# The products that only keep TensorE at work: three F32R products for each fp32 one

## The chip, the cores and the metric

The kernel runs on one core of one Trainium2 chip. The metric is the device time of one execution in microseconds; it is given as the median of several runs. [...] A product in fp32 runs on TensorE as two passes, each with its own weight load, and the trace shows both; a product in F32R (fp32 bits, rounded beforehand) is one pass.

## The reference, cut to what matters

Two parts, the second fed by the first, for 4 batches, 8 heads of 48, 768 steps, model width 384 and inner width 1024:

```python
f = 1.0 / (1.0 + np.exp(-f_logit))
for t in range(S):                                   # gated linear attention
    state = f[:, :, t, :, None] * state + np.einsum('bhd,bhe->bhde', k[:, :, t], v[:, :, t])
    y[:, :, t] = np.einsum('bhd,bhde->bhe', q[:, :, t], state)
...
k = np.maximum(xk @ w_k, 0.0)                        # xk, xr: x mixed with the step before
v = k * k @ w_v
r = 1.0 / (1.0 + np.exp(-(xr @ w_r)))
return (r * v).astype(np.float32)
```

## The kernel before

**Work.** The attention runs in 24 chunks of 128 steps (`YA`, `YB`, `SP`, `TR` or `QT` and others are the TensorE tasks of a chunk: many small products of 64 x 64, lines 373, 393, 410, transposes at 344 and 351). Three chunks make a unit of 384 steps, and there are 8 units. A unit's mixing network is `F` (xk times w_k, 8 blocks), `R` (xr times w_r, 3 blocks) and `W` (squares times w_v, 6 half blocks), all in `mm3` at line 558: each fp32 operand is split into a high and a low F32R part, and three products of 384 columns (high-high, high-low, low-high) stand for one.

**Weights.** They come as 64-bit words. For each piece DVE turns the words into fp32 in three steps (`S`, `T`, `X`: lines 678, 687, 690), ACT rounds the high part (`H`, line 693) and POOL subtracts it for the low part (`L`, line 697). `k.w["wv"]` is a pair of tiles, [0] for high and [1] for low parts, of 8 blocks of 384 columns. The last block of the second tile is filled by the pieces `wvL4` and `wvL5`, which run after 50 us.

**Order.** The string `ORDER` gives one sequence of all tasks, and `emit` pins each engine to it: an engine never runs a task ahead of one that stands before it. A token such as `+4s` is a filler: `fill` issues that many products of constants, whose result nobody reads. Its letter says into which part of PSUM they go: `y` (`py`), `s` (`pss`) or `m1` (tile 1 of `pm`). In order, the fillers are `+2y +1y +1y` in the first 12 us and `+1m1 +2s +4s +2m1 +1s` between 34 and 44 us: 14 fp32 products of 256 columns, for which the trace shows 28 passes.

**Start of the program.** DVE sets `sure`, `low` (a tile of 512 columns: column 0 of each block of 128 is 1, the rest 1e-18), `py` and `pss`. Then it starts on `sf0.0` (line 463), which waits for the first DMA of `f`.

**Names in the steps below.** `zb` (line 330) and `T` (336) are DVE steps of the attention's state, after `SP` (lines 373 and 393) of their chunk. `F0.0` is the first block of unit 0's network: the first product of line 558 in the trace. It needs a PSUM tile that the weight piece `wv3` leaves at its `X` step (line 690).

Of the kernel before, what the change touches and what calls it, by code (L numbers as in the profile page):

```python
# [17 lines left out]
DM, DFF = 384, 1024  # L18
P = 128
# [7 lines left out]
NF = DFF // P  # L27
# [165 lines left out]
FL = "p a c -> p (a c)"  # L193
# [3 lines left out]
class Rwkv:  # L197
# [554 lines left out]
    def fill(self, what):  # L752

        count, bank = int(what[0]), what[1:]
        to = (self.py[:, 0, 256:] if bank == "y" else self.pss[:, 0, :256] if bank == "s"
              else self.tiles["pm"][int(bank[1:])][:, :256])
        for _ in range(count):
            self.nc.tensor.matmul(to, self.low[:, 0], self.low[:, 1:3], start=False, stop=True, skip_group_check=True)

    def add_start(self, pl):  # L760
        nc = self.nc
# [64 lines left out]
@with_exitstack  # L826
def rwkv_kernel(ctx: ExitStack, tc: tile.TileContext, zt, qkt, vt, wk, wr, wv, mu, cst, gen, out):
    nc = tc.nc
    k = Rwkv(nc, tc)
    k.zt, k.qkt, k.vt, k.wk, k.wr, k.wv, k.mu, k.cst = zt, qkt, vt, wk, wr, wv, mu, cst  # L830
    cp = ctx.enter_context(tc.tile_pool(name="cp", bufs=1))
    pm = ctx.enter_context(tc.tile_pool(name="pm", bufs=1, space=bass.MemoryType.PSUM))


    k.f_t = [cp.tile([P, UC, NP, C], F32, name=f"f{i}") for i in range(NFB)]
    k.qk_t = [cp.tile([P, 2, NP, C], F32, name=f"qk{i}") for i in range(NQ)]
    k.ident = cp.tile([P, P], F32, name="ident")
    k.tri = cp.tile([P, P], F32, name="tri")
    k.sure = cp.tile([P, 1], F32, name="sure")
    k.mask = cp.tile([P, C // 2], F32, name="mask")  # L840
    k.mu_sb = cp.tile([P, 2, KJ], F32, name="mu_sb")
    k.one_mu = cp.tile([P, 2, KJ], F32, name="one_mu")
    k.z_t = [[cp.tile([P, NP, 64], F32, name=f"z{i}{h}") for h in (0, 1)] for i in range(2)]
    k.done = cp.tile([P, 2], F32, name="done")
    k.sm = cp.tile([P, NP, D], F32, name="sm")
    k.low = cp.tile([P, NP, C], F32, name="low")
    k.g_t = cp.tile([P, 2, NP], F32, name="g")
    k.bl = cp.tile([P, N, NP], F32, name="bl")
    k.w = {
        n: [cp.tile([P, a, b], F32R, name=f"{n}{i}") for i in (0, 1)]  # L850
        for n, a, b in (("wk", KJ, DFF), ("wr", KJ, DM), ("wv", NF, DM))
    }

    k.pss = pm.tile([P, 2, 512], F32, name="pss")

    k.py = pm.tile([P, 2, 512], F32, name="py")
    k.least = cp.tile([P, 15], F32, name="least")
    k.flag = cp.tile([1, 1], I32, name="flag")
    k.tiles = {
        tag: [  # L860
            (pm if tag == "pm" else cp).tile([P] + shape, F32R if tag[:2] in ("xh", "xl") else F32, name=f"{tag}{i}")
            for i in range(n)
        ]
        for tag, (n, shape) in BUFS.items()
        if not tag.startswith("k2")
    }

    k.turns = ctx.enter_context(tc.tile_pool(name="turns", bufs=1))
    k.words = {
        tag: k.turns.tile([P, KJ, 2 * P, 2], I32, name=f"words_{tag}", tag=tag) for tag in BUFS if tag.startswith("k2")  # L870
    }
    nc.scalar.preload_act_table_set(EXP_SET)
    nc.vector.memset(k.sure, FULL)
    for r in (0, 64):
        nc.vector.memset(k.sure[r : r + D], SURE)
    nc.vector.memset(k.low, LOW)
    nc.vector.memset(k.low[:, :, 0:1], 1.0)
    nc.vector.memset(k.py[:, :, :], 0.0)
    nc.vector.memset(k.pss[:, :, 256 : 256 + NP * D], 0.0)
    for t in (*k.z_t[0], *k.z_t[1]):  # L880
        nc.gpsimd.memset(t[:, :, D:], 0.0)

    plan = Plan()
    k.add_start(plan)
    k.add_all(plan, lambda u, t: out[u // NU, u % NU * UT + t * P : u % NU * UT + t * P + P, :])
    k.emit(plan.schedule())
    with tc.If(k.strong > 0):
        general(k, gen, out)
# [121 lines left out]
```

## Time and profile before

| | |
|---|---|
| median of 3 runs | 341.58 us (341.30 to 341.67) |
| the profiled execution | 341.73 us |
| its span, first to last instruction | 339.9 us |
| mean granted clock of TensorE | 0.999 |
| PE / DVE / ACT / POOL busy | 94% / 75% / 60% / 45% |

The profiled execution is 1.8 us longer than its span, and 0.15 us above the median. Times in the rows below count from the start of the span.

### The profile page before, as it was taken

The numbers are of one execution on the slowest core, as the hardware profiler recorded it, in microseconds if no ns is written. First come the engines' busy times: TensorE is split into PE (matmuls) and PEld (weight loads), VectorE is DVE, ScalarE is ACT, GpSimd is POOL, SyncE is SP. The second block draws the span as 40 slices with busy tenths as digits, with TensorE's granted clock in tenths as the row PEclk, the third lists the DMA queues.
The fourth block names the chain that finished last, engine by engine and source line by source line (L and its number), as shares of the span: only waits on it lengthen the run. The fifth ranks groups of instructions, "written<-read, shape, count | busy, mean of one in ns | idle before, by whom it ended". The sixth has DMA issues, their size and how long they took to land. (4 is left out here: it accounts for less than half of the span.)

```text
span 339.9 us, 10992 instructions
## 1 busy us (share of the span) xinstructions
PE 320.8 (94%) x4574; PEld 304.5 (90%) x4574; DVE 255.5 (75%) x519; ACT 205.2 (60%) x432; POOL 153.4 (45%) x194
## 2 busy tenths in 40 slices
PE   4795889999999999999999999999999999999993
PEld 4675678899999999999999999999999999999993
DVE  5997999999988987686998886787475627837420
ACT  3888788784887736783658648591858236133420
POOL 2369589847762435313653356525612405214300
PEclk9999999999999999999999999999999999999999
DMA  7999667015465234470257122541520133040002
GB/s 230 398 385 360 185 193 273 14 29 158 175 198 152 75 97 153 102 267 25 87 125 269 62 46 85 170 143 60 187 91 5 32 117 92 35 141 23 0 4 79
DMA packets 20347, 45.24 MB, mean 133 GB/s; under 512 B 2752, under 2 KB 12736, under 8 KB 20288
## 3 DMA queue, kind: packets, MB, share of 16 engines
q1 hardware_dynamic: 20144, 44.25, 39.4%
q8 instruction: 38, 0.62, 0.8%
q10 hardware_dynamic: 144, 0.20, 0.2%
q14 instruction: 21, 0.17, 0.2%
HBM read 38.54 MB, written 4.72 MB: 127 GB/s over the span
## 5 line engine op out<-in xcount | busy, mean ns | idle before, releaser
L558 PE MATMUL pm<-xh,wk 128*128 128x384 f32 x384 | 103.5, 341 | 0.7 <-DVE words L690 0.5
L558 PE MATMUL pm<-wv,k2h 128*128 128x384 f32 x384 | 98.4, 338 | 0.0
L596 POOL TENSOR_TENSOR k2l<-kk,k2h 128x384 fp32r<-128x384 f32 x44 | 46.4, 1059 | 63.6 <-DVE kk L588 24.9
L558 PEld LDWEIGHTS pm<-xh,wk 128*128 128x128 f32 x384 | 69.8, 188 | 2.3 <-DVE words L690 0.6
L558 PEld LDWEIGHTS pm<-wv,k2h 128*128 128x128 f32 x384 | 69.0, 188 | 0.9 <-issue 0.5
L558 PE MATMUL pm<-wv,k2l 128*128 128x384 f32 x192 | 64.5, 336 | 0.4 <-issue 0.4
L558 PE MATMUL pm<-xl,wk 128*128 128x384 f32 x192 | 64.5, 336 | 0.0
L550 POOL TENSOR_TENSOR xl<-xm,xh 128x384 fp32r<-128x384 f32 x35 | 37.4, 1075 | 32.2 <-DVE xh L544 27.8
L289 POOL TENSOR_TENSOR qk<-qk,rb 128x256 f32<-128x256 f32 x23 | 17.1, 742 | 60.6 <-ACT rb L275 33.1
L586 ACT ACTIVATE k2h<-r 128x384 fp32r<-128x384 f32 x64 | 32.2, 519 | 12.8 <-DVE r L582 12.4
L558 PE MATMUL pm<-wr,xh 128*128 128x384 f32 x144 | 37.1, 339 | 0.3 <-DVE words L690 0.3
L558 PEld LDWEIGHTS pm<-wv,k2l 128*128 128x128 f32 x192 | 36.1, 188 | 0.0
L558 PEld LDWEIGHTS pm<-xl,wk 128*128 128x128 f32 x192 | 36.0, 188 | 0.0
L581 ACT ACTIVATE r<-pm 128x384 f32<-128x384 f32 x41 | 20.0, 488 | 24.5 <-PE pm L558 22.2
L558 PEld LDWEIGHTS pm<-wr,xh 128*128 128x128 f32 x144 | 25.8, 188 | 0.8 <-DVE words L690 0.6
L443 ACT ACTIVATE x<-py 64x128 f32<-64x128 f32 (+1 forms) x69 | 21.4, 310 | 8.1 <-PE py L410 4.9
L535 DVE SCALAR_TENSOR_TENSOR xm<-pm,mu_sb,x 128x384 f32<-128x384 f32 x42 | 24.9, 609 | 0.6
L270 DVE TENSOR_TENSOR_SCAN pm<-f,low 128x512 f32<-128x512 f32 x18 | 25.0, 1387 | 0.5 <-ACT f L624 0.3
L590 ACT ACTIVATE kk<-r 128x384 f32<-128x384 f32 x38 | 19.4, 519 | 9.6 <-DVE r L582 7.1
L558 PE MATMUL pm<-wr,xl 128*128 128x384 f32 x72 | 24.2, 336 | 0.0
L410 PE MATMUL py<-qk,z 64*64 64x64 f32 x704 | 21.6, 227 | 1.7 <-DVE z L330 0.9
L582 DVE TENSOR_SCALAR r<-pm 128x384 f32<-128x384 f32 x23 | 12.4, 549 | 12.8 <-PE pm L558 12.1
(129 smaller groups left out, 575.6 us busy)
## 6 DMA issues: line engine op xcount, KB each, us to landing
qk<-in_qkt SPq DMA_DIRECT2D x24, 512.0 KB, 5.6
words<-in_wv SPq DMA_DIRECT2D x12, 512.0 KB, 4.8
f<-in_zt SPq DMA_DIRECT2D x7, 768.0 KB, 6.7
v<-in_vt SPq DMA_DIRECT2D x24, 192.0 KB, 2.9
out<-o SPq DMA_DIRECT2D x23, 192.0 KB, 3.4
words<-in_wk SPq DMA_DIRECT2D x6, 512.0 KB, 5.0
words_k2l<-in_wk SPq DMA_DIRECT2D x4, 384.0 KB, 7.2
words_k2h<-in_wk SPq DMA_DIRECT2D x4, 384.0 KB, 7.6
```

Of the source, the lines that this page charges most:

```text
L270: pl.add(f"b{i}", ga, ("V", 1.25, 1, lambda: nc.vector.tensor_tensor_scan(b().rearrange(FL), f().rearrange(FL), self.low.rearrange(FL), 1. ...
L289: e.tensor_tensor(k()[:, ::2], k()[:, ::2], rb()[:, ::2], op=ALU.mult)
L410: first[c, h] = nc.tensor.matmul(to, lhs, rhs, start=(c, h) not in first, stop=stop, skip_group_check=True)
L443: e.activation(o, i_, AF.Copy, scale=sign)
L535: pl.add(f"xm{u}.{n}{j}", pr, ("V", 0.62, 0, lambda xm=xm, n=n, j=j: nc.vector.scalar_tensor_tensor(xm(), pm("d", u, j)[:, :UT], self.mu_s ...
L550: e.tensor_tensor(lo(), xm(), hi().bitcast(F32), op=ALU.subtract)
L558: nc.tensor.matmul(ps, lhs(a, j), rhs(bb, j), start=ends[0] and i == 0, stop=ends[1] and i == len(pr) - 1)
L581: pl.add(f"r{u}.{f}", kf, ("A", 0.5, 0, lambda r=r, ps=ps: nc.scalar.activation(r(), ps(), AF.Relu)), ("V", 0.56, 0, lambda r=r, ps=ps: nc ...
L582: ("V", 0.56, 0, lambda r=r, ps=ps: nc.vector.tensor_scalar(r(), ps(), 0.0, None, op0=ALU.max)),
L586: pl.add(f"h{u}.{f}", kf, ("A", 0.53, 0, lambda r=r, hi=hi: nc.scalar.activation(hi(), r(), AF.Square)), after=[f"r{u}.{f}"], **kw)
L590: ("A", 0.53, 0, lambda r=r, kk=kk: nc.scalar.activation(kk(), r(), AF.Square)),
L596: e.tensor_tensor(lo(), kk(), hi().bitcast(F32), op=ALU.subtract)
```

## The change

Each filler's fp32 product of `low` becomes three F32R products on a slice of the second tile of `wv`, 256 columns each and into the same place. DVE copies 384 columns of `low` into that slice at the start, between the memsets of `low` and of `py`.

```diff
-        for _ in range(count):
-            self.nc.tensor.matmul(to, self.low[:, 0], self.low[:, 1:3], start=False, stop=True, skip_group_check=True)
+        spare = self.w["wv"][1][:, NF - 1]
+        for _ in range(3 * count):
+            self.nc.tensor.matmul(to, spare[:, :P], spare[:, P:], start=False, stop=True, skip_group_check=True)
...
     nc.vector.memset(k.low[:, :, 0:1], 1.0)
+    nc.vector.tensor_copy(k.w["wv"][1][:, NF - 1], k.low.rearrange(FL)[:, :DM])
     nc.vector.memset(k.py[:, :, :], 0.0)
```

## Rows read from the trace of the kernel before

**Rows 1.** The page, part 1: busy us, share of the span, instructions.

```profile
PE 320.8 (94%) x4574; PEld 304.5 (90%) x4574; DVE 255.5 (75%) x519; ACT 205.2 (60%) x432; POOL 153.4 (45%) x194
```

**Rows 2.** Windows: us, engines' busy us (instructions), granted clock, DMA share, GB/s.

```profile
47.15:335.00 287.85, 286.27 (x3778) 276.38 (x3778) 215.75 (x435) 170.63 (x358) 127.25 (x150) 1.00 0.34 106
...
34.50:47.11 12.61, 10.37 (x268) 7.99 (x267) 12.40 (x24) 9.55 (x21) 7.83 (x10) 1.00 0.67 215
```

**Rows 3.** Timeline, 27 to 48 us: start, us, instruction, idle before it and releaser.

```profile
27.25 0.34 PE L373 MATMUL pss<-qk 64*64 64x64 f32 x8 [0.98 <-issue]
...
28.08 0.36 DVE L330 TENSOR_TENSOR z<-pss,z 128x192 f32<-128x192 f32 x1 [0.79 <-PE pss L393]
...
33.45 0.51 PE L373 MATMUL pss<-qk 64*64 64x64 f32 x19 [2.38 <-issue]
...
34.50 0.36 DVE L330 TENSOR_TENSOR z<-pss,z 128x192 f32<-128x192 f32 x1 [1.98 <-POOL qk L290]
...
47.16 0.44 PE L558 MATMUL pm<-xh,wk 128*128 128x384 f32 x1 [0.48 <-DVE words L690]
```

**Rows 4.** Windows from one stall of PE to the next, and on.

```profile
27.24:33.44 6.20, 3.82 (x127) 3.27 (x126) 4.42 (x10) 4.73 (x14) 5.93 (x9) 1.00 0.94 366
33.44:45.49 12.05, 10.23 (x253) 7.93 (x253) 10.82 (x21) 10.19 (x21) 7.56 (x10) 1.00 0.69 220
45.49:112.41 66.92, 65.56 (x1016) 61.71 (x1017) 63.28 (x119) 51.11 (x108) 43.73 (x50) 1.00 0.45 144
112.41:245.04 132.63, 132.62 (x2040) 128.27 (x2040) 105.86 (x218) 82.93 (x180) 60.58 (x76) 1.00 0.37 117
```

**Rows 5.** Line 758, the fillers: ns min/median/max, first and last start.

```profile
L758 PE MATMUL pss<-low x14: 379/379/483, 35.8 to 43.9; 128*128 128x256 f32 x14
...
L758 PE MATMUL py<-low x8: 379/508/634, 5.1 to 11.6; 128*128 128x256 f32 x8
...
L758 PE MATMUL pm<-low x6: 379/379/483, 34.3 to 41.4; 128*128 128x256 f32 x6
```

**Rows 6.** Timeline of PE, 37 to 43 us.

```profile
37.17 1.89 PE L758 MATMUL pss<-low 128*128 128x256 f32 x8
...
42.72 0.46 PE L410 MATMUL py<-qk,z 64*64 64x64 f32 x16 [0.93 <-DVE z L330]
```

**Rows 7.** Timeline of DVE, the first 4 us.

```profile
2.91 0.38 DVE L879 MEMSET pss<- 128x384 f32 x1
...
3.61 0.49 DVE L463 TENSOR_SCALAR f<-f,sure 128x512 f32<-128x512 f32 x1 [0.32 <-DMA f<-in_zt]
```

**Rows 8.** Line 544, DVE's copies of 384 columns from fp32 to F32R.

```profile
L544 DVE CAST xh<-xm x26: 344/356/1184, 44.6 to 307.4; 128x384 fp32r<-128x384 f32 x26
```

**Rows 9.** Timeline of PE, 109 to 113 us.

```profile
109.31 0.62 PE L558 MATMUL pm<-wv,k2h 128*128 128x384 f32 x2
...
111.51 0.51 PE L558 MATMUL pm<-wv,k2h 128*128 128x384 f32 x2
112.42 0.34 PE L558 MATMUL pm<-wv,k2l 128*128 128x384 f32 x1 [0.40 <-issue]
```

**Rows 10.** Windows of short stretches with many small products.

```profile
107.40:109.31 1.91, 1.91 (x132) 1.83 (x128) 1.20 (x3) 1.88 (x3) 0.00 (x0) 1.00 0.76 225
241.08:243.00 1.92, 1.92 (x131) 1.85 (x133) 1.11 (x4) 1.49 (x4) 1.57 (x3) 1.00 0.24 87
241.46:245.04 3.58, 3.58 (x138) 3.50 (x135) 2.35 (x6) 2.32 (x7) 3.23 (x7) 1.00 0.21 54
80.12:83.85 3.73, 3.73 (x128) 3.41 (x129) 3.62 (x5) 0.61 (x2) 2.43 (x4) 1.00 0.52 198
...
107.63:112.41 4.78, 4.39 (x142) 4.17 (x135) 4.30 (x10) 4.75 (x4) 0.00 (x0) 1.00 0.82 249
```

**Rows 11.** Timeline of SP's DMA issues, near 237 us.

```profile
237.32 0.38 SPq L234 DMA_DIRECT2D qk<-in_qkt  x1
```

**Rows 12.** The page, part 6: DMA issues, KB each, us from issue to landing.

```profile
qk<-in_qkt SPq DMA_DIRECT2D x24, 512.0 KB, 5.6
```

## The prediction

> **What bounds the kernel now.** I read the page's busy line first: PE is at work 94% of the span and no other engine over 75% [rows 1]. That is a mean over two stages, so I cut the span at F0.0, the first product of the network. From 47.15 to 335 us PE is busy 286.27 of 287.85 us [rows 2]: there the kernel is PE's own work, end to end. Whatever moves F0.0 moves the end by as much, and so does every new pause of PE behind it; the fillers themselves all lie ahead of it.
>
> Next: what starts F0.0? In the timeline it waits for DVE's last step on weight piece wv3 [rows 3]. DVE is busy 12.40 of the 12.61 us before that [rows 2], so this is a full queue that began at 34.50 with zb3. And zb3 had DVE idle for 1.98 us [rows 3]. The view names POOL, which had long been done; zb3 reads what SP3 puts into PSUM, and SP3 is the group of line 373 that broke off in the middle and went on at 33.45, after 2.38 us of "issue", a wait with no releaser [rows 3]. So the chain of the first stage is: pause of PE, SP3, zb3, a full DVE queue, F0.0.
>
> What are these pauses? A group breaks off in its middle at 27.25, 33.45, 45.50 and 112.42. From the first to the second the windows count 127 + 126 = 253 instructions of PE, to the third 253 + 253 = 506, to the fourth 1016 + 1017 = 2033 [rows 4]. With 3, 6 and 15 semaphore instructions of PE's queue, which the view leaves out, these are 1, 2 and 8 times 256. PE gets its program in blocks of 256 instructions and pauses when it is through one before the next has come. From 27.25 to 33.45, with the DMA engines 94% busy, that took 6.20 us [rows 4]; the block that ended in the pause at 112.42 took 4.78 us, at a DMA share of 0.82 [rows 10]; one passed without a pause in 3.58 us, at 0.21 [rows 10].
>
> **The change part by part.** *The copy.* DVE's casts of the same shape took 0.34 to 1.18 us, 0.36 in the middle [rows 8]. DVE was idle 0.32 us for the first load of f after its memsets [rows 7], so sf0.0 comes 0.03 to 0.86 us late; I take 0.1, by the median. It hides in DVE's later idle times of 0.79 and 1.98 us before zb2 and zb3, both ended by PE's blocks [rows 3]. Without that cover it would cost its 0.1.
>
> *The fillers' time.* Eight passes took 1.89 us, so one costs (1.89 - 0.38) / 7 = 0.216 us and an fp32 product 0.43 us [rows 5, 6]. No row has an F32R product of 256 columns. One of 384 with its own weight load takes 0.51 - 0.336 = 0.175 us (two of them take 0.51) [rows 9]; by columns alone 256 would take 0.117. So three cost 0.35 to 0.52 us; I take 0.36, as the columns set the pace of the passes before too. The nine fillers after SP3 and before zb4's wait (1, 2, 4 and 2) save 0.6 us of PE, or cost up to 0.8. Neither reaches F0.0: behind them PE waits 0.93 us for DVE [rows 6], and DVE is the full queue. I cost it at zero. [...]
>
> *The instruction count.* This is what I think decides. Each filler was two passes and two loads, four instructions; three F32R products are three and three, six. The 28 passes [rows 5] are 14 fillers, so PE's program grows by 28 instructions: 8 before SP2, 28 before F0.0. Every later border of a block falls that much earlier in the work.
>
> At 27.25 and 33.45 the border moves 8 instructions, four small products, forward. When a block comes depends on the full DMA queues, not on PE, so I keep 33.45. Four more products stand behind the pause: (0.51 - 0.22) / 18 = 16 ns each [rows 3], 0.22 us being one's own length as the view draws it, together 0.07 us. zb3, and so F0.0, come **0.07 us later**. At 45.50, 28 more instructions come behind the pause, about 0.2 us, and PE had 0.48 us to spare before F0.0 [rows 3]: zero.
>
> At 112.42 the border moves to the product at 109.31: between them lie 14 products and 14 loads [rows 9]. The pause there, 112.42 less the 111.86 at which the product was due (111.51 and two of 0.175), 0.56 us, **goes away: -0.56**. But the new block is just the burst of 128 small products from 107.40 to 109.31, which PE is through in 1.91 us [rows 10]; no block of before was nearly as short. What is late next is the block behind it. If a block is asked for as its predecessor starts, it came 4.8 us after that in the old case; the start moves only 0.23 us (107.63 to 107.40), and the pause would be 4.8 - 1.9 = 2.9 us. If the queue runs some instructions ahead, the request comes 28 instructions earlier at the pace before the burst, where a product and its load take 0.175 us: 14 x 0.175 = 2.4 us. The block then comes by 112.42 - 2.4 = 110.0, a pause of up to 0.7 us, or none if it finds the DMA queue empty. I take the second, since nearly all borders pass without a pause, and of its 0 to 0.7 about the middle, **+0.4**.
>
> Sixteen blocks on (4080 instructions counted from 112.42 to 245.04, 16 blocks with semaphore instructions [rows 4]) the same happens: the border at 245.05 moves into the end of the burst of chunk 20, and the new block takes 1.92 instead of 3.58 us [rows 10]. Bounds: without a lead it came by 245.05 at the latest, less 0.38, so a pause up to 1.7 us; with one, none. But 0.5 MB of qk is issued at 237.32 and takes 5.6 us to land, until 242.9 [rows 11, 12]; a request behind it comes about then, and some tenths pass until PE goes on. I take **+0.6** past the 243.00 where PE needs it.
>
> Of the other blocks, with borders moved by 28, the tightest one beside DMA traffic passes in 3.73 us, from 80.12 [rows 10]: up to 4.78 - 3.73 = 1.05 us if it came as slowly as the one at 112.42. The 3.58 us that passed without a pause are nearer: zero.
>
> [...]
>
> *Sum:* 0.07 - 0.56 + 0.4 + 0.6 = +0.5 us on the profiled 341.73 (span 339.9 and 1.8 around it), 342.2; against the median of 341.58, which lies 0.15 lower, **342.1 us**. I count 0.2%, 0.68 us, as what a measurement tells from no change, so this is still "same", near its upper edge of 342.26.
>
> **Rivals.** *Requests have no lead* (slower). Place: the blocks after 109.31 and 243.00. Price: 2.9 - 0.56 = 2.3 and 1.7 us, 345.6 together, 343.3 with the second alone. It decides from the point where either new pause passes 1.2 us. For it: the old pause at 112.42 shows that a block can take 4.8 us. Against: PE's queue seldom starves at the other borders. 13%.
>
> *All borders are hidden:* the old pause goes, no new one comes: 0.07 - 0.56, 341.1 us. For it: both new requests fall in stretches where PE is slow, 2.4 us earlier. Against: qk's load in front of them. [...] 20%.
>
> *The early block comes at another time.* A request before SP3 that gets ahead of a data load, or behind it, moves 33.45. Each 0.1 us earlier is worth 0.1 at the end, until DVE's 1.98 us of idle are gone (339.6); later costs the same. For it: the DMA engines are 94% full there. Against: the request moves by under 0.1 us. 10% earlier, 340.6 as a middle; 7% later, 342.6 to 343.6.
>
> *The clock falls* in 34 to 47 us, as F32R keeps PE busy for less. PE came out of 2.38 us of idle at 33.45 at full pace (16 ns a product), and its longest idle would grow from 0.93 to about 1.5 us. A few us of line 558 at half pace would cost 2 or more: 343.6. 3%. [...]
>
> *The rest,* 47%, is my forecast, with 341.5 to 342.6 as its own range.
>
> **How the numbers follow.** Faster than 340.9 is most of the early-block gain and a little of the rest: 0.12. Slower than 342.26 are the missing lead, the later block, the clock and a third of the forecast: 0.37. The other 0.51 is same. The range leaves out the deeper part of the early gain and the full price of missing leads: 340.8 to 343.3.
>
> **What would show it.** The fillers: 42 F32R passes, six in 0.7 us or so. Pauses named "issue" near 27.2, 33.4, 109.3 and 243.0, none at 112.4; zb3 near 34.57; F0.0 near 47.2; PE full behind it. I am wrong if the pause at 33.45 moves by more than 0.3 us, if 109.3 and 243.0 show no pause or one over 1.2 us, or if F0.0 waits for PE.

## The result, and the profile after

The changed kernel takes 343.33 us (median of 13 runs, 342.32 to 345.22), the kernel before 341.30 (13 runs): a ratio of 1.0064, with a 95% interval from 1.0048 to 1.0080. So it is slower, by about 2.0 us (1.6 to 2.7). I had forecast 342.1 and a range up to 343.3; the time lies just past its end. The sign of the sum was right and its size was not.

The profiled execution took 343.52 us. Its page, part 1 (PE is TensorE, PEld its weight loads, DVE is VectorE, ACT ScalarE, POOL GpSimd; SPq below is SyncE's queue), against [rows 1], and its line of the fillers (min/median/max ns, first and last start), against [rows 5]:

```profile
PE 322.4 (94%) x4588; PEld 308.3 (90%) x4588; DVE 255.2 (75%) x520; ACT 205.0 (60%) x432; POOL 154.1 (45%) x194
```

```profile
L759 PE MATMUL pss<-wv x21: 278/282/387, 37.2 to 45.4; 128*128 128x256 f32 x21
...
L759 PE MATMUL py<-wv x12: 279/415/562, 5.0 to 12.2; 128*128 128x256 f32 x12
...
L759 PE MATMUL pm<-wv x9: 278/280/386, 35.8 to 42.7; 128*128 128x256 f32 x9
```

PE has 14 products and 14 loads more than before, and the 42 F32R passes are there, as forecast. The window from F0.0 to the start of the last product of line 558, after and then before, and PE's timeline after show where the time went:

```profile
48.66:335.92 287.26, 286.08 (x3778) 276.61 (x3778) 215.22 (x434) 170.56 (x358) 126.93 (x150) 1.00 0.33 106
```

```profile
47.16:333.98 286.82, 285.93 (x3777) 276.36 (x3778) 215.66 (x434) 170.62 (x358) 127.24 (x150) 1.00 0.34 106
```

```profile
28.43 0.59 PE L373 MATMUL pss<-qk 64*64 64x64 f32 x11 [2.12 <-issue]
...
34.89 0.62 PE L373 MATMUL pss<-qk 64*64 64x64 f32 x25 [1.14 <-issue]
...
38.42 1.68 PE L759 MATMUL pss<-wv 128*128 128x256 f32 x12
...
48.66 0.44 PE L558 MATMUL pm<-xh,wk 128*128 128x384 f32 x1 [1.26 <-DVE words L690]
...
110.25 0.63 PE L410 MATMUL py<-ss,v 64*48 64x64 f32 x32
111.29 0.51 PE L558 MATMUL pm<-wv,k2h 128*128 128x384 f32 x2 [0.41 <-issue]
...
243.95 0.62 PE L410 MATMUL py<-ss,v 64*48 64x64 f32 x29
244.90 0.31 PE L410 MATMUL py<-ss,v 64*48 64x64 f32 x3 [0.33 <-issue]
245.14 0.44 PE L558 MATMUL pm<-xh,wk 128*128 128x384 f32 x1
```

The reader is to see four things. The old pause at 112.42 [rows 9] is gone. Two new ones stand at 111.29 and 244.90, where the text expected them: each is the end of a burst of small products, and everything in this trace is 1.5 us later than in that of before. F0.0 is at 48.66 instead of 47.16 [rows 3], as both early pauses end later. And from F0.0 on the same work takes 287.26 us, where before takes 286.82 for the same stretch (47.16 to 333.98). Of this execution's 1.9 us, then, 1.5 came ahead of F0.0 and 0.4 behind it. One execution can mislead: in the next section the same program has F0.0 at 47.37.

### The profile page after: what moved, and what is told of

Same layout as the page of the kernel before. It is cut to its first block, busy times and chain, and to the rows that moved or that the text cites. A ratio compares the mean times of both kernels' runs of the same rounds, so it can differ in the third digit from the quotient of the medians.

```text
span 341.8 us, 11020 instructions
## 1 busy us (share of the span) xinstructions
PE 322.4 (94%) x4588; PEld 308.3 (90%) x4588; DVE 255.2 (75%) x520; ACT 205.0 (60%) x432; POOL 154.1 (45%) x194
```

## The experiments

Two ways to name a cause were open. **The blocks:** 28 more PE instructions move the borders of the 256-instruction blocks, and the moved blocks come late. **The work:** the F32R products themselves, by their time, by the clock, or by DVE's copy. Below, "behind F0.0" is the stretch from F0.0 to the start of the last product of line 558, and the size of a pause is worked out from starts. In a burst that isn't interrupted, the first product of line 558 starts 0.56 us after the last group of line 410 in that burst (0.58 near 84 us, where the group is cut otherwise); what it starts later is the pause.

**1. The changed kernel once more** (no edit), for the scatter between executions.

> The changed kernel once more, for a second profile and as the yardstick on this chip. Both theories: about 2 us slower than before, of which 0.4 us behind F0.0 (pauses of PE near 111.3 and 244.9, lengths 0.5 and 0.55). Borders theory (28 more instructions move the borders of PE's 256-instruction blocks): the block in SP2 comes at 28.0 or later, whatever the granted clock shows. Clock theory (F32R fillers keep PE at work for less, the clock falls): a profile without stretches at half clock between 10 and 32 us has F0.0 within 0.3 us of 47.16.

Measured: 342.97 us against 341.60, ratio 1.0048 [1.0028, 1.0068]. The table of PE's waits and PE's timeline, in this execution:

```profile
PE pss L373 <- issue: 3.7, 2, 2.5
PE py L410 <- issue: 1.6, 3, 0.7
...
PE pm L558 <- issue: 0.5, 1, 0.5
```

```profile
83.68 0.66 PE L410 MATMUL py<-ss,v 64*48 64x64 f32 x27
84.60 0.27 PE L410 MATMUL py<-ss,v 64*48 64x64 f32 x2 [0.26 <-issue]
84.80 0.44 PE L558 MATMUL pm<-xh,wk 128*128 128x384 f32 x1
...
109.43 0.63 PE L410 MATMUL py<-ss,v 64*48 64x64 f32 x32
110.52 0.51 PE L558 MATMUL pm<-wv,k2h 128*128 128x384 f32 x2 [0.47 <-issue]
...
243.17 0.62 PE L410 MATMUL py<-ss,v 64*48 64x64 f32 x29
244.38 0.31 PE L410 MATMUL py<-ss,v 64*48 64x64 f32 x3 [0.59 <-issue]
244.62 0.44 PE L558 MATMUL pm<-xh,wk 128*128 128x384 f32 x1
```

Here F0.0 is at 47.37, near the old 47.16, and the loss lies behind it: 288.08 us. A third pause has appeared, at 84.60, the end of the block that the prediction had costed at zero. The three are 84.80 - 83.68 - 0.58 = 0.54, 110.52 - 109.43 - 0.56 = 0.53 and 244.62 - 243.17 - 0.56 = 0.89 us.

The expectation for the blocks missed in one place: the one in SP2 came at 27.18, not at 28.0 or later. So the 1.5 us ahead of F0.0 in the first trace are no fixed price of the moved borders. F0.0 within 0.3 us of 47.16, in a trace whose page has the granted clock at 90% or more in every slice up to 34 us, is what the clock theory had; the loss behind F0.0, where the granted clock is 1.00, it doesn't explain.

**2. Two F32R products for each fp32 one:** four instructions a filler, as before, so no border moves.

```diff
-        for _ in range(3 * count):
+        for _ in range(2 * count):
```

> Two F32R products for each fp32 one instead of three: 4 instructions per filler as before, so every border stands where it stood, and PE's work in a filler is 0.24 us instead of 0.43. Borders theory: no change against before within 0.3%, pauses at 27.25, 33.45, 45.5 and 112.4 as before. Clock theory: PE does even less than with three, so as slow as the changed kernel or slower, 343 us or more, with half-clock stretches in the profile.

Measured: 342.30 against 341.60, 1.0016 [0.9997, 1.0036], and no pause behind F0.0; its waits name only the two early ones:

```profile
PE pss L373 <- issue: 3.4, 2, 2.7
```

```profile
47.80:333.95 286.15, 285.72 (x3778) 276.30 (x3778) 215.49 (x434) 170.31 (x358) 127.37 (x150) 1.00 0.33 107
```

286.15 us is what the work behind F0.0 takes without these pauses; the old one near 112.4, expected as before, is missing too. F32R fillers and the copy, with every border in its place, make no loss that can be told; the interval leaves room for up to 0.36%.

**3. One fp32 product of 192 columns and one F32R of 256 for each filler:** six instructions, as in the changed kernel, with more of the old fp32 work.

```diff
-        for _ in range(3 * count):
+        for _ in range(count):
+            self.nc.tensor.matmul(to[:, :192], self.low[:, 0], self.low.rearrange(FL)[:, P : P + 192], start=False, stop=True, skip_group_check=True)
             self.nc.tensor.matmul(to, spare[:, :P], spare[:, P:], start=False, stop=True, skip_group_check=True)
```

> Each filler is one fp32 product of 192 columns and one F32R product of 256: 6 instructions as in the changed kernel, 0.44 us of PE as before. Borders theory: as slow as the changed kernel, ratio 1.006 to before. Clock theory: as fast as before, but for the 0.4 us behind F0.0.

Measured: 343.49 against 341.60, 1.0051 [1.0030, 1.0073]; behind F0.0 287.70 us, with pauses of 0.70 at 85.1, 0.29 at 110.8 and 0.61 at 244.4. The loss comes with six instructions a filler, though half of them are fp32 work as before.

**4 and 6. A part of the fillers.** Only the four early ones become F32R (borders 8 instructions earlier), or only the ten later ones (20 earlier).

```diff
+        for _ in range(count if bank != "y" else 0):
+            self.nc.tensor.matmul(to, self.low[:, 0], self.low[:, 1:3], start=False, stop=True, skip_group_check=True)
-        for _ in range(3 * count):
+        for _ in range(0 if bank != "y" else 3 * count):
```

(for the other part, the two conditions change places)

> F32R products for the four fillers of the first 12 us alone, fp32 for the ten after 34 us: 8 more instructions, so borders are 8 earlier everywhere. If the loss lies ahead of 34 us (both theories say so): 1.3 to 1.6 us slower than before, F0.0 near 48.6. If it lies in the ten late fillers: F0.0 within 0.2 us of 47.16 and no change.

> F32R products for the ten fillers after 34 us alone, fp32 for the four early ones: borders are 20 earlier behind F0.0 and where they were ahead of 34 us. Borders theory: pauses behind F0.0 at two or three of the places of the changed kernel, 287.2 us or more from first to last product of line 558, and 1 to 2 us slower than before. If the changed kernel's loss needs the early fillers as well: no change.

Measured: early only 341.31 against 341.60, 0.9998 [0.9983, 1.0014], with no pause behind F0.0 (286.25 us); late only 342.60 against 341.70, 1.0033 [1.0017, 1.0049], with 287.00 us behind F0.0 and one pause, at 243.49, one product behind the end of a burst (243.49 - 242.61, less the 0.28 of that step elsewhere: 0.60 us). Both expectations missed in part: 4 lost nothing, so eight more instructions ahead of 34 us make no loss, and 6 shows one pause where two or three were expected. What the step of 28 costs is no straight line in the count: 8 cost nothing that can be told, 20 about half. What counts is which borders fall at the end of a burst or just behind it.

**5. One F32R product for each fp32 one:** the least PE work of all, and borders 28 instructions later.

```diff
-        for _ in range(3 * count):
+        for _ in range(count):
```

> One F32R product for each fp32 one: 2 instructions per filler, 28 fewer than before, so borders fall 28 later in the work, and PE's work in a filler is 0.12 us. Borders theory: behind F0.0 no border lies near the end of a burst any more, so no pauses there: first to last product of line 558 in 286.2 us (286.8 before, 287.3 to 288.1 in the changed kernel), and a time like that of the kernel before or up to 0.6 us better. Clock theory: the least work of all, so the slowest, 343 us or more.

Measured: 342.17 against 341.70, 1.0018 [1.0003, 1.0033]. Its profiled execution took 347.59 us, 5.4 above the median and 4.0 above the next of 13. In it PE waits 3.06 us, named "issue", before 102.68, in the middle of a burst, so against the expectation a block can come late at these borders too; one execution doesn't say how often. The kernel with the least filler work loses less than half of what the changed kernel loses, so a loss of the clock through lazier fillers isn't what decides.

**7. The copy alone:** the kernel before, with DVE's copy.

```diff
+        spare = self.w["wv"][1][:, NF - 1]
...
+    nc.vector.tensor_copy(k.w["wv"][1][:, NF - 1], k.low.rearrange(FL)[:, :DM])
```

> The copy on DVE alone, fillers as before: no border moves. Both theories: within 0.2% of before. More than 0.5 us would say that the copy's 0.35 us travels to F0.0, against what the prediction took.

Measured: 342.03 against 341.70, 1.0007 [0.9991, 1.0022]; the old pause at 112.68, behind F0.0 286.56 us. The copy costs nothing that can be told.

**8. Fewer fp32 fillers:** the kernel before with 9 of its 14, borders 20 instructions later.

```diff
-        for _ in range(count):
+        for _ in range((count + 1) // 2):
```

> The kernel before with 9 of its 14 fp32 fillers (of two or four in a row only half): 20 instructions fewer, borders 20 later, nothing of the change in it. Borders theory: no pauses behind F0.0, 286.2 us from first to last product of line 558, time as before or up to 0.6 us better. Clock theory: PE works less, so half-clock stretches and a slower kernel.

Measured: 342.14 against 341.70, 1.0013 [1.0000, 1.0025]; no pause behind F0.0 (286.26 us), F0.0 at 48.17. Inconclusive on the small scale: its interval ends at no change.

**9. Only the count:** the kernel before, without copy and without F32R fillers, with 14 tiny products (28 instructions, 64 x 64) after the filler `+2m1`, behind SP3.

```diff
+        for _ in range(7 if what == "2m1" else 0):
+            self.nc.tensor.matmul(to[:64, :64], self.low[:64, 0, :64], self.low[:64, 1, :64], start=False, stop=True, skip_group_check=True)
```

> The kernel before, fp32 fillers and no copy, with 28 instructions more (seven fp32 products of 64 x 64 behind the filler at 41 us, where PE waits 0.9 us anyway; their result is read by nobody). No F32R filler, no border moved ahead of 37 us. Borders theory: pauses behind F0.0 near 84.5, 110.5 and 244.4, 287.3 to 288.1 us from first to last product of line 558, and 1.0 to 1.5 us slower than before. If the loss comes from the F32R products or from the early borders: no change.

Measured: 343.48 against 341.69, 1.0052 [1.0028, 1.0076]. The window behind F0.0 and PE's timeline:

```profile
47.90:335.89 287.99, 286.24 (x3777) 276.63 (x3778) 216.18 (x434) 170.53 (x358) 128.52 (x151) 1.00 0.33 106
```

```profile
84.20 0.66 PE L410 MATMUL py<-ss,v 64*48 64x64 f32 x27
85.28 0.27 PE L410 MATMUL py<-ss,v 64*48 64x64 f32 x2 [0.42 <-issue]
85.48 0.45 PE L558 MATMUL pm<-xh,wk 128*128 128x384 f32 x1
...
110.11 0.63 PE L410 MATMUL py<-ss,v 64*48 64x64 f32 x32
110.98 0.50 PE L558 MATMUL pm<-wv,k2h 128*128 128x384 f32 x2 [0.25 <-issue]
...
243.63 0.62 PE L410 MATMUL py<-ss,v 64*48 64x64 f32 x29
244.82 0.31 PE L410 MATMUL py<-ss,v 64*48 64x64 f32 x3 [0.58 <-issue]
245.07 0.44 PE L558 MATMUL pm<-xh,wk 128*128 128x384 f32 x1
```

The same three pauses (0.70, 0.31, 0.88 us) and the same loss, from 28 instructions alone. The 14 products keep PE busy for 1.0 us, all of it ahead of F0.0, for which PE still waits 0.61 us.

**10 and 11. The load in front of the block.** I took each of the three late blocks to be asked for just behind a load of qk of 512 KB (chunks 9, 12 and 23); no view shows when a block is asked for. Here those three loads bring an eighth (64 KB), in the changed kernel and in the kernel before; the three chunks then compute on what the buffer held, and only the time is of use.

```diff
-        pl.add(f"qk{i}", ga - 0.3, ("Q", 1.42, 1, lambda: nc.sync.dma_start(self.qk_t[i % NQ], self.qkt[i])),
+        pl.add(f"qk{i}", ga - 0.3, ("Q", 1.42, 1, lambda: nc.sync.dma_start(*(t[:, :1, :1] if i in (9, 12, 23) else t for t in (self.qk_t[i % NQ], self.qkt[i])))),
```

> The changed kernel with the qk loads of chunks 9, 12 and 23 cut to an eighth (64 of 512 KB; these chunks then work on old data, and their output is left wrong). Theory that a block's request waits its turn behind the load issued just before it: the blocks come earlier, the pauses near 84.6, 110.5 and 244.4 vanish, 286.2 us from first to last product of line 558, and 1.2 to 1.9 us faster than the changed kernel, near 341.7. Theory that a block of nothing but small products cannot be refilled in time whatever the DMAs do: pauses as in the changed kernel, 343.

> The same three loads cut in the kernel before, as the control for it (the same chunks work on old data). If the smaller loads only act through the blocks: at most the pause of 0.4 to 0.6 us near 112.4 goes, so 0 to 0.5 us faster than before. If less DMA traffic is worth something by itself: as much faster as the changed kernel becomes.

Measured: the changed kernel with small loads 341.33 against 341.69, 0.9990 [0.9970, 1.0011]; the kernel before with small loads 341.89, 1.0009 [0.9993, 1.0025]. The windows behind F0.0, changed kernel first:

```profile
47.47:333.72 286.25, 285.77 (x3778) 276.36 (x3778) 215.68 (x434) 170.32 (x358) 127.34 (x150) 1.00 0.32 102
```

```profile
47.16:333.72 286.56, 286.04 (x3778) 276.32 (x3778) 215.24 (x434) 170.50 (x358) 127.68 (x151) 1.00 0.32 102
```

All three pauses are gone, and with them the loss, while the same cut gives the kernel before nothing. The DMA view shows how. First the changed kernel of experiment 1, whose load was issued at 237.59: from 237.5 to 241.9, and from 241.9 to 243.5. Columns: queue, kind: packets, MB, share of the 16 engines; and the load's us to landing.

```profile
q1 hardware_dynamic: 478, 0.97, 82.7%
...
qk<-in_qkt SPq DMA_DIRECT2D x1, 512.0 KB, 5.1
...
q1 hardware_dynamic: 98, 0.14, 25.2%
q8 instruction: 1, 0.02, 3.8%
```

And the changed kernel with small loads, from 236.7 to 239.9 and from 239.9 to 241.2:

```profile
q1 hardware_dynamic: 571, 0.65, 67.0%
...
out<-o SPq DMA_DIRECT2D x2, 192.0 KB, 3.6
qk<-in_qkt SPq DMA_DIRECT2D x1, 64.0 KB, 3.2
...
q8 instruction: 1, 0.02, 4.6%
q1 hardware_dynamic: 4, 0.01, 1.8%
```

The one packet of the instruction queue comes when the data in front of it are nearly through: after 241.9 behind the large load, of which 0.14 MB were still to come and which landed at 237.59 + 5.1 = 242.7, and between 239.9 and 241.2 behind the small one. In the first case PE starts the last product of its block at 243.59 (243.17 + 0.62, less the 0.20 of a product's own length) and waits until 244.38; in the second the same place comes near 242.8, and the block is there.

**12. The kernel before once more,** as a control.

> The kernel before once more, for a second profile: ratio 1.000. It shows how far F0.0 and the pause near 112.4 scatter without any change; by the profiles so far F0.0 between 46.9 and 48.0, a pause of 0.3 to 0.6 us or none at 112.4, none at 84.6 or 244.4.

Measured: 341.65 against 341.69, 1.0007 [0.9985, 1.0028]; behind F0.0 286.49 us, with the old pause at 111.62.

## Why the prediction was wrong, point by point

**That the count decides, and not the fillers: right.** Experiment 9 gives the whole loss by the count alone, 2 none that can be told with the F32R fillers and the old count.

**The step that failed: "The 3.58 us that passed without a pause are nearer: zero".** The block from 80.12, for which the text had a bound of 1.05 us, isn't free. It cost 0.01, 0.54, 0.70 and 0.70 us in the four profiles with 28 more instructions (the changed kernel twice, 3 and 9), 0.49 in the mean. Loads of 512 KB are issued shortly before it, as before the one at 243.00 (here `words` and `qk`, issued at 77.87 and 78.25 in experiment 1), and I looked for such a load only at 243.00. In the one profile of four without this pause, the first of after, the block came ahead of these loads: there the view from 79.1 to 80.9, just behind their issue at 79.14 and 79.53, has the packet of the instruction queue.

```profile
q1 hardware_dynamic: 176, 0.33, 74.8%
q8 instruction: 1, 0.02, 3.7%
```

In experiment 1 there is none from 78.3 to 82.3, while loads pass, and one from 82.3 to 83.4:

```profile
q1 hardware_dynamic: 320, 1.07, 82.4%
```

```profile
...
q8 instruction: 1, 0.02, 5.4%
```

By the packets' own times in the traces it starts 31.1 us behind F0.0 in the first of after, and 35.0 us in experiments 1, 3 and 9. Why the packet was ahead that once is open.

**The other terms behind F0.0,** as means of the same four profiles: the new pause near 110 us 0.40 (forecast 0.4); the one near 244 us 0.75 (forecast 0.6); the old one, which goes, 0.32 in the four profiles of kernels with the old borders and fp32 fillers (before, 7, 11 and 12: 0.56, 0.32, 0.16, 0.24) where I took the 0.56 of one trace. So I took too much gain from a pause that scatters. The sum of pauses becomes 0.49 + 0.40 + 0.75 - 0.32 = +1.3 us in place of 0.4 + 0.6 - 0.56 = +0.44. With the 0.07 ahead of F0.0 the forecast's own sum would have been 343.0 us. The stretch behind F0.0 agrees: 287.26, 288.08, 287.70 and 287.99, in the mean 287.76, against 286.82, 286.56, 286.56 and 286.49, in the mean 286.61: +1.15.

**F0.0 +0.07 us: neither shown nor contradicted.** The first trace of after has +1.50, but the same program has +0.21 in experiment 1, and experiment 9, whose program up to SP3 is that of before, has F0.0 at 47.90. The step that the 0.07 was for, from the end of the pause in SP3 to zb3, took 1.08 us in the first trace of after and 1.14 to 1.30 in experiments 1, 3 and 10, against 1.04 or 1.05 in before, 7, 11 and 12. Kernels 10 and 11 differ in the whole change and took 341.33 and 341.89 us, so what lies ahead of F0.0 costs nothing that the medians can tell. The chain itself held: from zb3 to F0.0 it is 48.66 - 35.97 = 12.69 us after, against 47.16 - 34.50 = 12.66 before [rows 3]. DVE's row for zb3 after:

```profile
35.97 0.36 DVE L330 TENSOR_TENSOR z<-pss,z 128x192 f32<-128x192 f32 x1 [0.67 <-POOL x L488]
```

**The 0.36 us of three F32R products: right.** The twelve at 38.42 give (1.68 - 0.28) / 11 = 0.127 us each, three 0.38. They reach no path, as forecast. The copy took 0.35 us, and sf0.0 started at 3.63 instead of 3.61 [rows 7]:

```profile
2.79 0.35 DVE L879 CAST wv<-low 128x384 fp32r<-128x384 f32 x1
...
3.63 0.49 DVE L463 TENSOR_SCALAR f<-f,sure 128x512 f32<-128x512 f32 x1
```

**The rivals.** That requests have no lead fell: its prices of 2.9 and 1.7 us were not seen (at most 0.53 and 0.89), and with the small load the packet near 244 started at 240.12, 0.7 us before PE entered the block ahead of that border (240.8, counted back by 256 instructions). That the early block comes at another time did happen in the first trace of after: the pause at 33.45 ended at 34.89, beyond the 0.3 us that I had named as a sign of being wrong. It is a scatter that needs no change, for it ended at 33.49 to 33.91 in experiments 1, 3, 9 and 10, and at 33.45 to 34.32 in before, 7, 11 and 12. That all borders are hidden fell: of the 29 or 30 borders behind F0.0 (3778 products and 3778 loads, 256 to a block) nearly all pass without a pause, and the two or three behind a large load don't. That the clock falls, as F32R keeps PE busy for less: that link was an assumption of mine, which no run shows, and experiments 2 and 5, with less filler work still, speak against it as the cause. That the early blocks come by the DMA queues and not by PE stays my estimate from the DMA share of 94% [rows 4]: no run changed a load ahead of 34 us.

**What stays open.** By the medians the changed kernel loses 2.0 us, and once more 1.4; 343.48 - 341.33 = 2.15 us lie between experiments 9 and 10, measured on the same chip, and the loads that 10 cuts are all issued after 78 us. The eight profiles named above differ by 1.9 us of span in the mean: 1.15 behind F0.0, and 0.74 ahead of it, where F0.0 is at 48.66, 47.37, 47.73 and 47.90 against 47.16, 47.68, 47.16 and 46.71. Whether the change has a part in the 0.74 is open. Without the first trace of after it is 0.49, and experiment 10, with the whole change, has F0.0 at 47.47 and no loss. So the profiles place 1.15 us or so at the moved borders, and the rest of the loss at no place for sure. No version beat both kernels: those without pauses (2, 4, 8 and 10) are within the uncertainty of before, or slightly above it.

## What to carry to other kernels

On an engine that is the bound, an edit far ahead can cost time by its number of instructions alone: here 28 more in the first 44 us, worth 0.5% in experiment 9, put the borders of 256-instruction blocks at the ends of bursts at 84, 110 and 244 us. Before such an edit, go through the blocks that PE passes fastest (here in 1.9 to 4.8 us) and ask which large load (here 512 KB) was issued just before the block is due, at all of them and not at the one that stands out; and take a pause's size from several profiles. Keeping the count (two products for one, as in experiment 2) is the first thing to try when a change that ought to be free loses half a per cent; padding it to other borders is an idea that no run here tried.

## What the runs showed of the hardware that I had not expected

**A block of instructions came behind a load of data.** Its packet is 16 KB (0.62 MB in the 38 packets of that queue on before's page), yet in 4.4 us of experiment 1, from 237.5 to 241.9, in which the queue of loads had 82.7% of the 16 engines, the packet didn't come. That it came after 241.9, and that with 64 KB in place of 512 KB it came between 239.9 and 241.2 and the pause went, speaks for a block that waits for the load here; when the request was made no view shows.

**Why just the short blocks suffer.** At the pauses near 110 and 244 in the four profiles with 28 more instructions, 2.2 to 2.4 us lie between the packet's start and PE's going on (in experiment 1 the packet starts at 242.01 and ends at 242.97, and PE goes on at 244.38). PE passes the block ahead of such a border in 1.9 us [rows 10]. So here the packet has to start 0.3 to 0.5 us before PE enters that block (2.2 to 2.4 less 1.9): with the small loads it did, by 0.9 and 0.7 us, and with the large ones it started between 0.1 us before and 0.4 us behind the entry. The block ahead of the border near 84 us is passed in 3.7 us; there the packet started 2.1 us behind the entry in experiments 1, 3 and 9.

**Half the clock early on, with a price in some executions.** The mean granted clock of the profiled execution is 0.984 to 0.994 in 12 of the 14, of both kernels, and 0.997 and 0.999 in the other two (3 and before). Us by us, and behind a pause of PE, three of the 12 have it at 0.50: the first of after from 29 to 31 us (pause to 28.43), experiment 2 in the stretches from 36, 38 and 40 us (pause to 33.81), experiment 12 from 35 to 37 us. The first row is the changed kernel's, the second that of experiment 12, the unchanged kernel, which was no slower for it (F0.0 at 46.71):

```profile
29.00:30.00 1.00, 1.00 (x35) 0.91 (x28) 0.13 (x1) 0.00 (x0) 1.00 (x2) 0.50 1.02 397
```

```profile
35.00:36.00 1.00, 1.00 (x18) 0.52 (x16) 1.00 (x3) 0.98 (x2) 1.00 (x1) 0.50 0.19 35
```

In the first the half pace lay in SP2's products (11 in 0.59 us, against 0.39 in experiment 1), and may have had a share in that trace's late F0.0, which no run separates; the pages of before and of experiments 1, 9, 10 and 11 have the granted clock at 90% or more in every slice up to 34 us. In experiments 6, 8 and 9 zb3 started 1.65 to 1.67 us behind the end of the pause, 0.6 us more than the 1.04 or 1.05 of before, 7, 11 and 12. In experiment 9 the rest of SP3 ran at half the pace: (0.80 - 0.22) / 18 = 32 ns a product, against 16 in before. Its rows:

```profile
33.84 0.80 PE L373 MATMUL pss<-qk 64*64 64x64 f32 x19 [2.66 <-issue]
```

```profile
35.51 0.36 DVE L330 TENSOR_TENSOR z<-pss,z 128x192 f32<-128x192 f32 x1 [2.88 <-PE pss L393]
```

Not all of the 0.6 us travels: experiment 6 still has F0.0 at 47.15.
